# One transformer block on one core: K and Q stored in operand order, the softmax output's DMAs moved to GpSimd's queue, and the end of the program reordered

## The chip, the core and the metric

The program runs on one core of a Trainium2 chip. The metric is the device time of one execution in microseconds (us); the profiler's span, from the first to the last instruction, is given beside it. Engines are named as in the profile: PE is TensorE (PEld its weight loads), DVE is VectorE, ACT is ScalarE, POOL is GpSimd, SP is SyncE, which here only issues DMAs.

## What is computed

A block with modulated layer norms, 2048 rows (S) of 512 (D), attention with 32 heads of 16, and a gated feed-forward of 1792 (F), all in float32:

```python
def _A_ref(x, wqkv, wo):
    ...
    scores = jnp.einsum("bhqd,bhkd->bhqk", q, k) * scale
    p = _softmax(scores, axis=-1)
    o = jnp.einsum("bhqk,bhkd->bhqd", p, v)
    return (lambda x, *d: x.transpose(*d))(o, 0, 2, 1, 3).reshape(B, S, D) @ wo

def _B_ref(x, w_gate, w_up, w_down):
    g = _silu(x @ w_gate)
    u = x @ w_up
    return (g * u) @ w_down
...
h = _layernorm(x, axis=-1) * (1 + ca) + sa
x = x + ga * _A_ref(h, A_wqkv, A_wo)
h = _layernorm(x, axis=-1) * (1 + cb) + sb
x = x + gb * _B_ref(h, B_w_gate, B_w_up, B_w_down)
```

The six vectors sa to gb come from silu(c) @ w_mod.

## The kernel before

**Products in three terms.** Every float32 operand of the projections and the feed-forward is split into a high part and a rest (a cast, then a subtraction), and a product is the sum high·high + high·rest + rest·high. The scores do the same inside one matmul: 48 of its partitions hold, for each of a head's 16 numbers, three rows, (high, rest, high) for K and (high, high, rest) for Q; two more rows (ones in K, the negated maximum in Q) subtract the maximum.

**Projections (up to the first score).** For each of the four chunks of 512 rows the kernel normalizes, transposes and modulates x, and computes Q and K transposed and V. `proj_T` (L358) copies a bank into `prt` (high and rest) and stores it with one DMA (L370) to the DRAM tensors `qd` and `kd`, which are two planes, high and rest. `load_parts` (L398) brings a group of four heads back as operand rows: three row blocks times two partition halves are six DMAs of 16 partitions each, `kop` for K (2048 columns, three tiles in turn) and `qop` for Q (512 columns).

**Attention.** The work is cut into 32 units: unit u is chunk u // 8 of the queries and head group u % 8 (four heads). A unit has 16 steps, one for each block of 128 keys; a step has four score matmuls (L504, exponential on ACT at L506) and four matmuls for the row maximum of a later unit (L477, maximum on DVE at L479). A score and a maximum matmul use different halves of PE's rows and run side by side. The maxima run `LEAD` = 20 steps ahead, so the first maximum of unit u+2 is due in unit u, at its 14th step. The probabilities times V (`pv_step`, L519) fill one bank per unit, `banks[7]`; its last row of every head is the softmax's denominator.

**From the pv bank to the out projection.** When a unit ends (`close_unit`, L808), ACT copies the bank to `o` in two halves (L523). Then a chain follows, step by step from the list `due`: the denominators go by DMA to `dn` (L529), DVE inverts them (L533), they go to DRAM `d_dr` (L534) and come back over all partitions as `rb` (L539); POOL multiplies (L545), and the product goes to `o_dr` (L546). Once the last unit of a chunk is through, `load_o` (L646) loads the chunk's `oT` and `split_o` (L651) splits it on POOL; the out projection reads it. All these DMAs stand in SP's queue, which issues in order: while one waits for its data, nothing behind it is issued. K and Q loads, two DMAs at each step (`before`, L821), the feed-forward's weights (L639, L644) and the splitting of those weights during the first 124 steps (`split_weights`, L573) are in the same queue.

**Plain and filled steps.** The order on every engine is written by hand (no scheduler): the program order of the Python code is the order of each engine's queue. In `plain` only attention runs. In `filled` (L899) each two steps carry 12 more pairs of matmuls with 64 rows from the previous chunk's work (`LONG`, `SHORT` say how many terms go after each score), then six half steps of pv. A chunk's work is the out projection (4 `filled`), the second norm and its transposes (`turned`, L681, 2 `filled`), and then 14 gate-up jobs of two `filled` and 14 down jobs of one. It begins at the steps `STARTS` = 138, 267, 396. A gate-up job ends with tanh on ACT, two products on DVE and a split to `mid` on POOL (L746 to L754), which the down job reads (L706).

**The end.** The third chunk keeps its last six jobs (`KEEP`) for after the attention. There `whole` runs them in full rows (L714) between the links of the last unit's chain; then come `load_o`, `split_o`, the last out projection, the norm and the last chunk's feed-forward (L957 to L998).

**The clock.** The profile gives the clock that TensorE was granted in a stretch (PEclk, 1.00 is full).

Of the kernel before, what the change touches and what calls it, by code (L numbers as in the profile page):

```python
# [102 lines left out]
def block_kernel(ctx, tc, x, wqkv, wo, w_gate, w_up, w_down, c, w_mod, out):  # L103
# [27 lines left out]
    qd = dram.tile([2, D, S], F32, name="qd")  # L131
    kd = dram.tile([2, D, S], F32, name="kd")
# [225 lines left out]
    def proj_T(ci, w, m):  # L358
        def job():
# [3 lines left out]
            def post():  # L363
# [5 lines left out]
                dst = (qd, kd)[w][:, m * P:(m + 1) * P, ci * CW:(ci + 1) * CW].rearrange("r p s -> p r s")  # L369
                nc.sync.dma_start(dst, prt.bitcast(F32))  # L370
# [27 lines left out]
    def load_parts(dst, src, parts, g, c0, c1):  # L398
        for r, part in enumerate(parts):
            heads = src[part, g * 64:(g + 1) * 64, c0:c1].rearrange("(s b d) c -> b d s c", s=2, b=2)  # L400
            for b in range(2):
                nc.sync.dma_start(dst[64 * b + 16 * r:64 * b + 16 * r + 16].bitcast(F32), heads[b])
                yield

    def load_k0(ci):
        run(load_parts(kop[0][:, :, ci * CW:(ci + 1) * CW], kd, KPARTS, 0, ci * CW, (ci + 1) * CW))

# [43 lines left out]
    stored, posts = set(), []  # L451
# [8 lines left out]
    def load_k(u):  # L460
        return load_parts(kop[u % 3], kd, KPARTS, u % NG, 0, S)

    def load_q(u):
        ci, g = divmod(u, NG)
        qop[u] = pb.tile([P, 2, CW], F32R, name="qop", tag="qop", bufs=3)
        return load_parts(qop[u], qd, QPARTS, g, ci * CW, (ci + 1) * CW)

# [40 lines left out]
    def pv_step(i, half):  # L508
# [13 lines left out]
        if kt == 15:  # L522
            nc.scalar.copy(o_[u][:, cols], pv[u][:, cols])  # L523

    def out_a(u):
# [3 lines left out]
        nc.sync.dma_start(dn, o[16:P:32, :].rearrange("h (b e) -> h b e", e=16))  # L529
        return o, dn  # L530

    def out_b(u, o, dn):
        nc.vector.reciprocal(dn, dn)  # L533
        nc.sync.dma_start(d_dr[u].rearrange("h (b e) -> (h b) e", e=16), dn)  # L534
        return o,

    def out_r(u, o):
        rb = pf.tile([P, CW], F32, name="rb", tag="rb", bufs=1)
        nc.sync.dma_start(rb, d_dr[u][:, None, :].to_broadcast([4, 32, CW]))  # L539
        return o, rb  # L540

    def out_c(u, o, rb):
# [3 lines left out]
        nc.sync.dma_start(o_dr[ci, g], on)  # L546
        stored.add(u)
# [69 lines left out]
    class Chunk:  # L617
        def __init__(self, ci, x2, oT, hT):
# [10 lines left out]
            nc.sync.dma_start(self.x2, xd[:, 4 * ci:4 * ci + 4, :])  # L629
# [16 lines left out]
        def load_o(self):  # L646
            for k in range(NK):
                src = o_dr[self.ci, 2 * k:2 * k + 2].rearrange("g (h e) s -> (g h) e s", e=32)[:, 0:DH, :]
                nc.sync.dma_start(self.oT[1][:, k, :].bitcast(F32), src)
# [334 lines left out]
    for t in range(4):  # L984
        ch.normalize(t)
# [36 lines left out]
```

## Time and profile before

| | |
|---|---|
| Time, median of 3 runs | 2179.66 us (2170.13 to 2184.38) |
| The profiled execution | 2185.03 us; its span 2183.2 us |
| First score, last scores (L504) | 198.73 us, 1987.56 us from the span's start |
| Busy: PE, DVE, ACT, POOL | 1964.7, 1571.5, 1263.3, 317.2 us |
| Granted TensorE clock, mean | 0.94 |
| DMA | 261.21 MB, 120 GB/s; SP's queue took 48.4% of 16 engines' span |

PE is busy 90% of the span, but a share over the whole span says little here: the three stages have different limits, and a matmul at half clock counts as busy twice as long. So the page is only the start, and the stretches are read one by one: how long 16 steps last, what PE waited for, and what clock it had.

### The profile page before, as it was taken

The numbers are of one execution on the slowest core, as the hardware profiler recorded it, in microseconds if no ns is written. First come the engines' busy times: TensorE is split into PE (matmuls) and PEld (weight loads), VectorE is DVE, ScalarE is ACT, GpSimd is POOL, SyncE is SP. The second block draws the span as 40 slices with busy tenths as digits, with TensorE's granted clock in tenths as the row PEclk, the third lists the DMA queues.
The fourth block names the chain that finished last, engine by engine and source line by source line (L and its number), as shares of the span: only waits on it lengthen the run. The fifth ranks groups of instructions, "written<-read, shape, count | busy, mean of one in ns | idle before, by whom it ended". The sixth has DMA issues, their size and how long they took to land. (4 is left out here: it accounts for less than half of the span.)

```text
span 2183.2 us, 40914 instructions
## 1 busy us (share of the span) xinstructions
PE 1964.7 (90%) x16860; PEld 1176.5 (54%) x16860; DVE 1571.5 (72%) x2666; ACT 1263.3 (58%) x2330; POOL 317.2 (15%) x301
## 2 busy tenths in 40 slices
PE   7998977888978998999968999999979999897799
PEld 5764433333434665665434666665444466565587
DVE  5467977778867887888856888888867988741333
ACT  3223866667756665666746666666757766663100
POOL 2001233332011100110011101100011010011222
PEclk9998998889889999999988999999988999999899
DMA  8776566565344454434534545443532445224443
GB/s 244 198 162 115 112 179 176 138 182 150 48 124 105 92 108 117 118 95 83 111 60 98 124 110 114 106 98 79 118 79 41 84 108 110 97 93 146 173 174 116
DMA packets 90175, 261.21 MB, mean 120 GB/s; under 512 B 20252, under 2 KB 32540, under 8 KB 69116
## 3 DMA queue, kind: packets, MB, share of 16 engines
q1 hardware_dynamic: 88836, 258.06, 48.4%
q8 instruction: 133, 2.18, 0.5%
q10 hardware_dynamic: 1152, 0.52, 0.1%
q14 instruction: 54, 0.44, 0.1%
HBM read 203.82 MB, written 53.74 MB: 118 GB/s over the span
## 5 line engine op out<-in xcount | busy, mean ns | idle before, releaser
L479 DVE TENSOR_REDUCE mx<-bank 128x1 f32<-128x512 f32 x2048 | 1304.1, 685 | 354.1 <-PE bank L477 201.3
L477 PE MATMUL bank<-kop,qop 48*128 48x512 f32 x2048 | 804.9, 452 | 63.0 <-DMA kop<-kd 28.8
L504 PE MATMUL bank<-qop,kop 50*128 50x512 f32 x2048 | 800.4, 446 | 35.1 <-ACT pt__6232 L506 1.6
L504 PEld LDWEIGHTS bank<-qop,kop 50*128 50x128 f32 x2048 | 364.8, 191 | 366.1 <-issue 75.6
L477 PEld LDWEIGHTS bank<-kop,qop 48*128 48x128 f32 x2048 | 360.1, 192 | 96.4 <-issue 62.0
L706 PE MATMUL bank<-act,wgu 64*128 64x512 f32 x1920 | 305.7, 395 | 8.5 <-DMA wgu<-gu_dr 8.5
L706 PEld LDWEIGHTS bank<-act,wgu 64*128 64x128 f32 x1920 | 191.6, 189 | 43.0 <-issue 9.3
L545 POOL TENSOR_TENSOR on<-o,rb 128x512 f32<-128x512 f32 x32 | 41.0, 1280 | 811.8 <-DMA rb<-d_dr 378.6
L706 PE MATMUL bank<-wd,mid 64*128 64x512 f32 x912 | 151.1, 397 | 2.1 <-DMA wd<-wd_dr 1.5
L753 POOL CAST mid<-m 128x512 fp32r<-128x512 f32 x56 | 34.3, 612 | 678.6 <-DVE m L752 672.4
L706 PEld LDWEIGHTS bank<-wd,mid 64*128 64x128 f32 x912 | 96.6, 188 | 15.9 <-POOL mid L753 1.8
L208 PE MATMUL bank<-hT,wqs 128*128 128x512 f32 x384 | 97.1, 404 | 3.7 <-DVE prt L367 2.4
L750 DVE SCALAR_TENSOR_TENSOR q<-th,bank 128x512 f32<-128x512 f32 x56 | 38.1, 681 | 86.0 <-ACT th L746 86.0
L746 ACT ACTIVATE th<-bank 128x512 f32<-128x512 f32 x56 | 33.5, 599 | 113.5 <-PE bank L714 79.2
L706 PE MATMUL bank<-wgu,act 64*128 64x512 f32 x288 | 54.4, 439 | 42.6 <-POOL act L654 41.0
L208 PEld LDWEIGHTS bank<-hT,wqs 128*128 128x128 f32 x384 | 71.5, 191 | 26.2 <-issue 5.9
L754 POOL TENSOR_TENSOR mid<-m,mid 128x512 fp32r<-128x512 f32 x56 | 72.3, 1291 | 4.5
L765 DVE TENSOR_TENSOR x<-bank,x 128x512 f32<-128x512 f32 x84 | 54.2, 683 | 25.9 <-PE bank L706 17.5
L714 PE MATMUL bank<-kop,kop 128*128 128x512 f32 x240 | 60.5, 410 | 8.6 <-ACT kop L654 8.5
L706 PEld LDWEIGHTS bank<-wgu,act 64*128 64x128 f32 x288 | 31.5, 203 | 54.5 <-POOL act L654 44.1
L714 PEld LDWEIGHTS bank<-kop,kop 128*128 128x128 f32 x240 | 46.7, 197 | 21.5 <-ACT kop L654 11.0
L367 DVE TENSOR_TENSOR prt<-bank,prt 128x512 fp32r<-128x512 f32 x32 | 22.0, 689 | 46.9 <-ACT prt L365 46.9
(6246 smaller groups left out, 5131.9 us busy)
## 6 DMA issues: line engine op xcount, KB each, us to landing
kop<-kd SPq DMA_DIRECT2D x192, 256.0 KB
wgu<-gu_dr SPq DMA_DIRECT2D x48, 1024.0 KB
wd<-wd_dr SPq DMA_DIRECT2D x28, 1024.0 KB
gu_dr<-wgu SPq DMA_DIRECT2D x14, 1024.0 KB
qop<-qd SPq DMA_DIRECT2D x198, 64.0 KB
kd<-prt SPq DMA_DIRECT2D x16, 512.0 KB
qd<-prt SPq DMA_DIRECT2D x16, 512.0 KB
rb<-d_dr SPq DMA_DIRECT2D x32, 256.0 KB
```

What stands on the lines that cost most here:

```text
L208: nc.tensor.matmul(pt, lhs(a, k), rhs(b, k), start=(n == 0), stop=(n == 3 * nk - 1))
L477: nc.tensor.matmul(pm, qop[u][rows, s, qt * P:(qt + 1) * P], kop[u % 3][rows, s, kc * CW:(kc + 1) * CW], start=True, stop=True)
L479: nc.vector.tensor_reduce(mx[u][:, b, s, qt, kc:kc + 1], pm, op=ALU.max, axis=AX.X)
L504: nc.tensor.matmul(sp, kop[u % 3][rows, h // 2, kt * P:(kt + 1) * P], qop[u][rows, h // 2, :], start=True, stop=True)
L545: nc.gpsimd.tensor_mul(on, o, rb)
L706: nc.tensor.matmul(outs[e], lhs(e, a, k)[rows], rhs(b, k)[rows], start=(ph == 0 and j == 0), stop=(ph == 1 and j == z))
L714: nc.tensor.matmul(outs[e], lhs(e, a, k), rhs(b, k), start=(j == 0), stop=(j == z))
L746: nc.scalar.activation(th, outs[0], AF.Tanh, scale=0.5)
L750: nc.vector.scalar_tensor_tensor(q, th, 1.0, outs[0], op0=ALU.add, op1=ALU.mult)
L753: nc.gpsimd.tensor_copy(mid[:, 0, :], m32)
L754: nc.gpsimd.tensor_sub(mid[:, 1, :], m32, mid[:, 0, :].bitcast(F32))
L765: nc.vector.tensor_add(ch.x2[:, t, :], outs[e], ch.x2[:, t, :])
```

## The change

`qd` and `kd` become [D, 3, S]: a row of D holds its three operand rows next to each other. `proj_T` writes high and rest with one DMA and the second copy of the high part with another. `load_parts` then needs one DMA of 48 partitions for each partition half, two instead of six. The loads of unit u+2 no longer go out two DMAs at a step from unit u's second step on, Q first: K is issued whole right behind the last score of unit u-1, whose tile it takes, and Q one step later; the loads for unit 1 come three steps earlier and once (before they stood in the program twice), those for unit 2 before step 0. The five kinds of DMA of the chain from `o` to `oT`, and the output stores of the first three chunks, move to POOL's queue; the product comes one step earlier, and `load_o` and `split_o` too. The chunks' work begins at steps 141, 267 and 399, so that every `filled` covers an odd step and the even one after it; `LONG` puts its terms after the first six scores; in `filled` the bank is copied to `o` in one piece.

At the end, seven jobs are kept instead of six. The last chunk's tiles are set up 24 steps before the end, and the three quarters of its `oT` that are complete are loaded and split then, on POOL. After the last pv, `out_terms` runs 36 of the last out projection's 48 matmuls first; the other 12 follow after 44 matmuls of the kept jobs. Of the kept jobs 32 matmuls come between the norm and its transposes, and four weight tiles are loaded ahead instead of three.

The core of the diff:

```diff
-KEEP = 6
-KWIN = 34
-STARTS = (138, 267, 396)
-LONG = (0, 2, 2, 2, 2, 2, 2, 0)
+KEEP = 7
+REST = 30
+STARTS = (141, 267, 399)
+LONG = (2, 2, 2, 2, 2, 2, 0, 0)
-KPARTS = (0, 1, 0)
-QPARTS = (0, 0, 1)
...
-    qd = dram.tile([2, D, S], F32, name="qd")
-    kd = dram.tile([2, D, S], F32, name="kd")
+
+    qd = dram.tile([D, 3, S], F32, name="qd")
+    kd = dram.tile([D, 3, S], F32, name="kd")
...
-                dst = (qd, kd)[w][:, m * P:(m + 1) * P, ci * CW:(ci + 1) * CW].rearrange("r p s -> p r s")
-                nc.sync.dma_start(dst, prt.bitcast(F32))
+                dst = (qd, kd)[w][m * P:(m + 1) * P, :, ci * CW:(ci + 1) * CW]
+                nc.sync.dma_start(dst[:, 1 - w:3 - w, :], prt.bitcast(F32))
+                nc.sync.dma_start(dst[:, 2 * w, :], prt[:, 0, :].bitcast(F32))
...
-    def load_parts(dst, src, parts, g, c0, c1):
-        for r, part in enumerate(parts):
-            heads = src[part, g * 64:(g + 1) * 64, c0:c1].rearrange("(s b d) c -> b d s c", s=2, b=2)
-            for b in range(2):
-                nc.sync.dma_start(dst[64 * b + 16 * r:64 * b + 16 * r + 16].bitcast(F32), heads[b])
-                yield
+    def load_parts(dst, src, g, c0, c1):
+        heads = src[g * 64:(g + 1) * 64, :, c0:c1].rearrange("(s b d) r c -> b (d r) s c", s=2, b=2)
+        for b in range(2):
+            nc.sync.dma_start(dst[64 * b:64 * b + KR].bitcast(F32), heads[b])
...
-        if kt == 15:
+        if kt == 15 and by_halves:
+        elif kt == 15 and half:
+            nc.scalar.copy(o_[u], pv[u])
...
-        nc.sync.dma_start(dn, o[16:P:32, :].rearrange("h (b e) -> h b e", e=16))
+        nc.gpsimd.dma_start(dn, o[16:P:32, :].rearrange("h (b e) -> h b e", e=16))
...
-        nc.sync.dma_start(rb, d_dr[u][:, None, :].to_broadcast([4, 32, CW]))
+        nc.gpsimd.dma_start(rb, d_dr[u][:, None, :].to_broadcast([4, 32, CW]))
...
-        nc.sync.dma_start(o_dr[ci, g], on)
...
+        nc.gpsimd.dma_start(o_dr[ci, g], on)
...
-        def load_o(self):
-            for k in range(NK):
+        def load_o(self, ks=range(NK)):
+            for k in ks:
-                nc.sync.dma_start(self.oT[1][:, k, :].bitcast(F32), src)
-
-        def split_o(self, alone=False):
-            for k in range(NK):
+                nc.gpsimd.dma_start(self.oT[1][:, k, :].bitcast(F32), src)
+
+        def split_o(self, ks=range(NK), alone=False):
+            for k in ks:
...
+    def add_o(ch, t0, outs):
...
+    def out_terms(ch, t, pt, ks):
+        for k in ks:
+            for a, b in ((0, 0), (0, 1), (1, 0)):
+                nc.tensor.matmul(pt, ch.oT[a][:, k, t * P:(t + 1) * P], ch.wo[k // 2][:, b, k % 2, :],
+                                 start=(k == 0 and a == b == 0), stop=(k == NK - 1 and a == 1))
...
-                    nc.sync.dma_start(od[:, 4 * ch.ci + t, :], ch.x2[:, t, :])
+                    (nc.sync if ch.ci == last else nc.gpsimd).dma_start(od[:, 4 * ch.ci + t, :], ch.x2[:, t, :])
...
-            at(i + 5, lambda: out_c(u, *res.pop(u)))
+            at(i + 4, lambda: out_c(u, *res.pop(u)))
-                at(i + 6, lambda: chunks[u // NG].load_o())
-                at(i + 7, lambda: chunks[u // NG].split_o())
-
-    loads = []
+                at(i + 5, lambda: chunks[u // NG].load_o())
+                at(i + 6, lambda: chunks[u // NG].split_o())
...
-        u, kt = divmod(i, 16)
-        if kt == 1 and 1 <= u + 2 < NU:
-            loads.append(chain(load_q(u + 2), load_k(u + 2)))
-        for _ in range(2):
-            while loads and next(loads[0], loads) is loads:
-                loads.pop(0)
+
+        u, kt = divmod(i + 1, 16)
+        if 1 <= u and u + 2 < NU:
+            if kt == 0:
+                load_k(u + 2)
+            if kt == 1:
+                load_q(u + 2)
...
+            load_k(2)
+            load_q(2)
...
-        if i == -LEAD + 6:
-            loads.append(chain(load_k(1), load_q(1)))
-        before(i)
+        if i == -LEAD + 3:
+            load_k(1)
+            load_q(1)
...
-            pvs((HALVES[(w - 2) % 4] if done > 8 else 0) + (w == 4 * steps // WIN - 1))
+            pvs((HALVES[(w - 2) % 4] if done > 8 else 0) + (w == 4 * steps // WIN - 1), True)
...
-    def filled(places, work, tail=None):
+    def filled(places, work, tail=None, pairs=8):
...
-            bank, places = Turn(4, 5, 0), ALONE[places]
-        for r in range(8):
+            bank, places = Turn(4, 5, 0), ALONE.get(places, places)
+        for r in range(pairs):
-        pvs(6)
+        pvs(6, False)
...
+    def two_of(u):
+        return [kop[u % 3][:, e, :].rearrange("p (k c) -> p k c", k=NK) for e in range(2)]
+
+    def begin_last():
+        chunks[last] = ch = Chunk(last, v_flat[:, 0:4 * D].rearrange("p (t d) -> p t d", t=4), two_of(NU - 2),
+                                  two_of(NU - 1))
+        ch.load_wo([kop[(NU - 3) % 3][:, k, :].rearrange("p (b k d) -> p b k d", b=2, k=2) for k in range(NK // 2)])
+
+    at(n - 24, begin_last)
+    at(n - 13, lambda: chunks[last].load_o(range(NK - 1)))
+    at(n - 11, lambda: chunks[last].split_o(range(NK - 1)))
...
-            plain(n - done // 4 - 2 * KWIN)
+            plain(REST)
...
+    filled(none, iter(()), pairs=4)
...
-    pairs = [(0, 1), (2, 3), (4, 5)]
-        return [banks[b] for b in pairs[turn_n % len(pairs)]]
+        return [(banks[4], banks[5]), (banks[6], banks[7])][turn_n % 2]
...
-    room = [v_flat[:, 4 * D * e:4 * D * (e + 1)].rearrange("p (t d) -> p t d", t=4) for e in range(2)]
-    oT, hT = ([kop[u % 3][:, e, :].rearrange("p (k c) -> p k c", k=NK) for e in range(2)] for u in (NU - 2, NU - 1))
-    ch = Chunk(last, room[0], oT, hT)
-    ch.load_wo([kop[(NU - 3) % 3][:, k, :].rearrange("p (b k d) -> p b k d", b=2, k=2) for k in range(NK // 2)])
-    chp = chunks[last - 1]
+    ch, chp = chunks[last], chunks[last - 1]
+    ch.load_x2()
+    for t in range(4):
+        out_terms(ch, t, banks[t], range(NK - 1))
+        if t == 1:
+            res[NU - 1] = out_b(NU - 1, *res[NU - 1])
+        if t == 3:
+            res[NU - 1] = out_r(NU - 1, *res[NU - 1])
+    take(rest, 12)
+    out_c(NU - 1, *res.pop(NU - 1))
-    res[NU - 1] = out_b(NU - 1, *res[NU - 1])
+    ch.load_o((NK - 1,))
-    res[NU - 1] = out_r(NU - 1, *res[NU - 1])
-    take(rest, 10)
-    out_c(NU - 1, *res.pop(NU - 1))
+    ch.split_o((NK - 1,), True)
-    ch.load_o()
-    take(rest, 12)
-    ch.split_o(True)
-    take(rest, 6)
-    for t0 in (0, 2):
-        run(out_pair(ch, t0, two(), False))
-        hook()
+    for t in range(4):
+        out_terms(ch, t, banks[t], (NK - 1,))
+        if t % 2:
+            add_o(ch, t - 1, banks[t - 1:t + 1])
-    ch.nt = [room[1][:, 2 * k:2 * k + 2, :] for k in range(2)]
+    ch.nt = [v_flat[:, (4 + 2 * k) * D:(6 + 2 * k) * D].rearrange("p (t d) -> p t d", t=2) for k in range(2)]
+    take(rest, 32)
-    ch.ahead = 3
-    take(rest, 12)
-    for kk in range(NK // 2):
-        run(ch.turned([banks[6], banks[7]], kk))
-        hook()
-        take(rest, 8)
-    run(rest)
+    ch.ahead = 4
+    for kk in range(NK // 2):
+        run(ch.turned(banks[2 * kk:2 * kk + 2], kk))
+        hook()
+        take(rest, 12)
+    run(rest)
```

Three places show the order of instructions. **SP's queue in unit 1**, where K and Q of unit 3 are loaded (`kop_86` is the tile of units 0, 3, 6, and so on). Before:

```order
L402 DMA qop<-qd 16x2x512 x4
L577 DMA mid<-in_B_w_down 128x2x512
L402 DMA qop<-qd 16x2x512 x2
L534 DMA d_dr<-dn 128x16
L539 DMA rb<-d_dr 128x1x512
L402 DMA kop_86<-kd 16x2x2048 x6
L546 DMA o_dr<-on 128x512
```

and with the change:

```order
L584 DMA wo_dr<-wgu 128x2048
L576 DMA mid<-in_A_wo 128x2x512
L401 DMA kop_86<-kd 48x2x2048 x2
L401 DMA qop<-qd 48x2x512 x2
L584 DMA wo_dr<-wgu 128x2048
```

The links of unit 0's chain (`d_dr`, `rb`, `o_dr`) stood before and behind K in the queue; now none is in it, and K stands ahead of Q.

**POOL's queue at the end of the first chunk's units** (units 5 to 7), where the out projection's operand is made (`act_5528` and `act_5457` are the tile `oT`). Before:

```order
L581 CAST wd<-mid 128x1024
L582 TENSOR_TENSOR wd<-mid,wd 128x1024
L545 TENSOR_TENSOR on<-o,rb 128x512 x3
L654 CAST act_5527<-act_5528 128x512
L655 TENSOR_TENSOR act_5528<-act_5528,act_5527 128x512
```

and with the change (units 6 and 7):

```order
L546 DMA o_dr<-on 128x512
L529 DMA dn<-o 128x1x16
L534 DMA d_dr<-dn 128x16
L539 DMA rb<-d_dr 128x1x512
L545 TENSOR_TENSOR on<-o,rb 128x512
L546 DMA o_dr<-on 128x512
L650 DMA act_5457<-o_dr 128x1x512 x4
L655 CAST act_5456<-act_5457 128x512
L656 TENSOR_TENSOR act_5457<-act_5457,act_5456 128x512
```

Where POOL held one product for a unit, it now holds the whole chain in order, four DMAs and the product, and the four loads of `oT`.

**PE's queue after the last pv matmul** (`bank_70` is the pv bank). Before, from the last pv matmul to the first kept jobs, then the out projection:

```order
L519 MATMUL bank_70<-pt__20836,v_flat 32x256
L714 MATMUL bank_65<-act_16074,wgu 128x512
L714 MATMUL bank_65<-act_16075,wgu 128x512
L714 MATMUL bank_65<-act_16074,wgu 128x512 x2
L714 MATMUL bank_65<-act_16075,wgu 128x512
...
L714 MATMUL bank_67<-kop_1421,kop_86 128x512 x12
```

and with the change:

```order
L517 MATMUL bank_70<-pt__20533,v_flat 32x256
L742 MATMUL bank_63<-kop_1412,kop_86 128x512 x9
L742 MATMUL bank_64<-kop_1412,kop_86 128x512 x9
L742 MATMUL bank_65<-kop_1412,kop_86 128x512 x9
L742 MATMUL bank_66<-kop_1412,kop_86 128x512 x9
L715 MATMUL bank_69<-act_15861,wgu 128x512
...
L742 MATMUL bank_63<-kop_1412,kop_86 128x512 x3
```

Before, 60 matmuls of kept jobs ran ahead of the whole out projection (48, the rows with `kop_1421`); now 36 of those 48 come first and need nothing of the last two units.

More of the change, by code (lines that the diff above doesn't have):

```diff
@@ L450, in block_kernel @@
     qop, mx, pts, pv, o_, due, res = {}, {}, {}, {}, {}, {}, {}
-    stored, posts = set(), []
+    posts = []
     n = 16 * NU
@@ L460, in load_k @@
     def load_k(u):
-        return load_parts(kop[u % 3], kd, KPARTS, u % NG, 0, S)
+        load_parts(kop[u % 3], kd, u % NG, 0, S)
     def load_q(u):
@@ L802, in block_kernel @@
     ones_rows(1)
-    run(load_q(0))
+    load_q(0)
     take(late, 22)
@@ L957, in block_kernel @@
     for i, half in halves:
-        pv_step(i, half)
+        pv_step(i, half, False)
     after(n - 1)
```

48 lines of the change are left out of this document (24 added, 24 removed).

## Prediction

> **What bounds the kernel now.** The page comes first, and only as a warning.
>
> ```profile
> span 2183.2 us, 40914 instructions
> PE 1964.7 (90%) x16860; PEld 1176.5 (54%) x16860; DVE 1571.5 (72%) x2666; ACT 1263.3 (58%) x2330; POOL 317.2 (15%) x301
> ```
>
> PE leads, but a matmul at half clock counts double, so I read stretches instead: score matmuls (L504) in chosen windows, four to a step; the last three columns are clock, DMA share and GB/s.
>
> ```profile
> 198.70:593.00 394.30, 191.61 (x513) 91.91 (x513) 0.88 0.59 143
> 1669.80:1711.50 41.70, 22.78 (x66) 10.60 (x64) 1.00 0.39 62
> 700.00:800.00 100.00, 44.11 (x108) 18.99 (x108) 1.00 0.39 104
> ```
>
> The first row is the plain start, 128 steps in 394.3 us, 3.08 each. The second is one plain unit at full clock, 16 steps in 41.7 us, 2.61 each. The third is filled, 27 steps in 100 us, 3.70 each. So the start loses 394.3 - 8 x 41.7 = **60.7 us** against the kernel's own clean unit. The waits of PE there say why:
>
> ```profile
> PE bank L477 <- DMA kop<-kd: 24.5, 3, 14.6
> PE bank L477 <- DMA gu_dr<-wgu: 8.8, 1, 8.8
> PE bank L477 <- issue: 7.7, 1, 7.7
> ```
>
> All three are the first maximum of a new unit, which needs the unit's K (the names in the last two rows are only what ended near it). The waits make 41 us; the rest is the clock, 0.88 against 1.00. One unit shows what makes K late, SP's queue and then PE:
>
> ```profile
> 549.45 0.56 SPq L529 DMA_DIRECT2D dn<-o  x1
> 550.12 4.20 SPq L402 DMA_DIRECT2D qop<-qd  x6
> 556.94 0.34 SPq L534 DMA_DIRECT2D d_dr<-dn  x1
> 558.37 0.55 SPq L539 DMA_DIRECT2D rb<-d_dr  x1
> 558.96 2.85 SPq L402 DMA_DIRECT2D kop<-kd  x6
> 580.44 0.76 PE L477 MATMUL bank<-kop,qop 48*128 48x512 f32 x1 [3.81 <-DMA kop<-kd]
> ```
>
> K's tile was free near 544, its DMAs went out at 558.96, behind Q and the chain, and landed only near 580. The windows of all engines for that transfer and for weight loads over 128 partitions:
>
> ```profile
> 559.00:580.00 21.00, 17.63 (x175) 8.39 (x171) 18.78 (x32) 16.09 (x32) 1.28 (x1) 1.00 0.79 100
> 2062.00:2082.00 20.00, 20.00 (x83) 16.32 (x82) 5.27 (x8) 1.80 (x3) 5.72 (x6) 0.93 0.59 249
> ```
>
> 100 GB/s at a share of 0.79 against 249 at 0.59: loads to 16 partitions hold the DMA engines 3.3 times as long for a byte. Two faults, then: a late issue (some 15 us) and a slow transfer (some 20).
>
> **After the first chunk** the waits of PE (600 to 1989) name another place.
>
> ```profile
> PE bank L706 <- POOL act L654: 41.0, 3, 16.0
> PE bank L519 <- ACT o L523: 17.8, 33, 0.9
> PE bank L706 <- DMA wgu<-gu_dr: 8.5, 2, 4.9
> 612.00:640.00 28.00, 12.38 (x102) 6.71 (x100) 10.62 (x18) 8.69 (x16) 7.54 (x9) 0.70 0.58 111
> 1095.00:1123.00 28.00, 11.36 (x88) 6.01 (x90) 8.54 (x15) 7.09 (x14) 8.66 (x9) 0.70 0.57 92
> 1577.00:1602.00 25.00, 14.70 (x117) 8.32 (x115) 11.51 (x19) 8.57 (x16) 8.65 (x9) 0.80 0.35 76
> ```
>
> Three out projections wait 41.0 us for the split operand, and the clock stays at half a little longer. The chain of the second one, on SP and POOL:
>
> ```profile
> 1075.08 0.57 SPq L529 DMA_DIRECT2D dn<-o  x1
> 1083.87 0.34 SPq L534 DMA_DIRECT2D d_dr<-dn  x1
> 1088.76 0.55 SPq L539 DMA_DIRECT2D rb<-d_dr  x1
> 1102.38 1.26 POOL L545 TENSOR_TENSOR on<-o,rb 128x512 f32<-128x512 f32 x1 [48.01 <-DMA rb<-d_dr]
> 1104.05 9.43 SPq L649 DMA_DIRECT2D act<-o_dr  x4
> 1114.24 0.61 POOL L654 CAST act<-act 128x512 fp32r<-128x512 f32 x1 [10.60 <-DMA act<-o_dr]
> 1114.93 1.27 POOL L655 TENSOR_TENSOR act<-act,act 128x512 fp32r<-128x512 f32 x1
> ```
>
> From 1075 to 1114, 39 us, of which the small transfers `d_dr` (4.9) and `rb` (13.6) queue with 3 MB of x and weights.
>
> **The end**, two windows and three stalls of PE:
>
> ```profile
> 1991.40:2059.70 68.30, 45.07 (x164) 32.24 (x160) 20.47 (x49) 9.87 (x15) 13.03 (x14) 0.81 0.41 136
> 2059.70:2183.20 123.50, 118.48 (x504) 96.12 (x504) 38.69 (x56) 8.41 (x14) 26.75 (x28) 0.98 0.45 176
> 2017.42 3.34 PE L714 MATMUL bank<-kop,kop 128*128 128x512 f32 x6 [6.99 <-ACT kop L654]
> 2041.83 0.48 PE L686 MATMUL bank<-ident,v_flat 128*128 128x128 f32 x1 [4.46 <-ACT v_flat L678]
> 2059.74 4.60 PE L714 MATMUL bank<-kop,wgu 128*128 128x512 f32 x10 [6.27 <-DMA wgu<-gu_dr]
> ```
>
> In the second window a matmul takes 118.48 / 504 = 0.235 us. The first holds 144 such and 16 transposes, about 36 us of work in 68.3.
>
> **The change part by part**, against the span of 2183.2. *K and Q.* K goes out right behind the score that frees its tile, with nothing of the chain ahead. Its transfer is bounded by 1.57 MB at 249 GB/s, 6.3 us, and by the 20 us of now; two blocks of 48 partitions are nearer to the wide loads, so I take 8. Its first maximum is due 13 steps later, 34 us: even 20 us fit, and 14 more are left for a store of split weights that SP waits for. So the 60.7 us go, whichever bound holds, unless something new is late. That is POOL: in the start it splits weights, and now holds the chain too.
>
> ```profile
> 198.70:593.00 394.30, 338.66 (x3051) 151.11 (x3050) 317.05 (x544) 272.69 (x535) 112.45 (x90) 0.88 0.59 143
> ```
>
> 112.45 us in 334 would be 34%, more while it splits; its 90 operations take 1.25 us each and are issued three or four at a time, so `dn` can stand behind some 5 us of splitting, and DVE's reciprocal, which waits for `dn`, is due only two steps, 5.2 us, after it. What is queued behind that reciprocal on DVE are the maxima, four to a step, that PE's banks wait for. I charge 0 to 2 us for each of eight units, 5 in all (bound 16): **-56**. K waits later in the run: **-4**.
>
> *Out projections.* `d_dr` and `rb` leave the queue of the big loads. No row shows a DMA on POOL's queue; the nearest are the same transfers in the unit above, `d_dr` 558.37 - 556.94 = 1.4 us, and in this chain 4.9 and 13.6. I take 3 and 5. From the end of the pv bank that makes 5.2 us to the reciprocal, 3 for `d_dr`, 5 for `rb`, 1.3 for the product, 3 and 4 for the store and load of the `oT` quarters, 0.6 for the first cast, and 2 for issuing: 24 us instead of 39. The first cast is needed after 10.5 steps of 2.5 us (26 us) in the first chunk, 9.3 (23) in the second, 13.3 (33) in the third. So the second still waits, with splits of 1.9 us a quarter behind the first one, about 3 us. Of 41.0 and some 8 for the clock I take **-44** (bounds -49 and -15).
>
> *Filled.* Weight loads no longer stand behind the chain: 8.5 us and the clock after them, **-10** (0 to -18). One copy instead of two spares PE part of 17.8 us, but odd groups put the maximum's two DMAs on ACT into the middle of a filled group: **-3** (-12 to +8). Four filled steps become plain, 4 x (3.70 - 2.61): **-4**.
>
> *The end.* 24 matmuls more, 168 in all, 39.5 us and 2 for transposes. The last unit's chain, with the links just used but no steps to wait for (copy 0.6, `dn` 3, 3, 5, 1.3, 3, 4, cast and subtraction 1.3), takes 21 us and has 36 + 44 matmuls over it, 18.8 us; the norm has 32 (7.5 us, against the 4.46 now waited), the split after the transposes 44. I leave 10 us of stalls: 52 instead of 68, **-17** (-25 to -3).
>
> *Before the first score.* PE waits there once, and DMA is nearly full early on:
>
> ```profile
> PE bank L477 <- DMA qop<-qd: 6.6, 1, 6.6
> 40.00:100.00 60.00, 60.00 (x291) 48.13 (x290) 28.55 (x54) 16.82 (x30) 0.00 (x0) 1.00 0.84 228
> ```
>
> The second load of unit 1, which caused the 6.6, is gone; 32 more stores of 256 KB are new, half of them in that window: 4 MB on 13.7 would ask 0.84 x 1.3 = 1.09 of the engines, 6 us too much, hidden in part by four `prt` buffers. **-4** (-10 to +12).
>
> Sum: -56 - 4 - 44 - 10 - 3 - 4 - 17 - 4 = **-142**. The profiled execution took 2185.0 in all, 1.8 outside the span and 5.4 above the median; from the median, 2179.7 - 142 = **2038 us**.
>
> A rule speaks against the chain's new place. The Trainium skill, DMA: Bandwidth & Descriptors, section Latency and other measured facts, gives a first byte after about 1 us on GpSimd's path and 0.6 on SP's. By it five links would be 2 us longer, and my estimate of the sum 2 us higher, since only the second out projection is short of time. No row here shows it, and nothing above hangs on it.
>
> **The rivals.** *K is issued in time but SP is not free*: stores that wait for POOL's splits stand ahead of K for over 14 us, and half of the 56 stays. For it: SP's 23 stores of split weights are in that stretch; against it: its greatest waits there are the chain's,
>
> ```profile
> SPq L529 <- ACT o L523: 72.0, 4, 21.8
> SPq L546 <- POOL on L545: 48.8, 7, 11.9
> ```
>
> About 2068; chance 0.12.
>
> *The chain on POOL is no shorter*, since the same 16 DMA engines serve it and `rb` takes 13.6 us again: the out projections keep waiting for 30 of the 44, the end for 8 of the 17: about 2076; chance 0.14. For it: the share of 0.57 in the second window while `rb` crept. Against it: in the unit above `rb` was sent at a quiet moment and nobody waited for it. The Trainium skill states it as a rule (DMA: Bandwidth & Descriptors, Issuing engines are not separate DMA queues): all queues share the engines, and a second one saves only the issue.
>
> *POOL's queue becomes the bound*, the slower side: POOL waits in order for `d_dr` and `rb`, 4.9 + 13.6 = 18.5 us as in the chain above. A `mid` behind them (0.61 + 1.27) has two filled groups, 14.8 us, until a down job reads it; beyond 13 us of waiting each us stops PE, 5.6 x 17 units = 95 us, and in 15 plain units a late `dn` stops DVE's maxima, some 8 us each, 120. 2038 + 215 = about 2250. Against it: POOL waited as long for `rb` before (48.01 in the row) and no down job suffered. Chance 0.06.
>
> *The waits go but the time does not*: DVE (busy 317.05 of 394.3 us already in the slow start) or the clock set a pace near 3 us a step, and the clean unit was an exception; about 2165, chance 0.07. Against it: that unit has DVE in the same work at 2.61.
>
> **How the numbers follow.** The forecast has 0.61, with 2005 to 2070 of its own. With the first two rivals the range is **2000 to 2100**. Three runs of before lie within 0.7%, so 1% is about what can be told from no change: faster 0.61 + 0.12 + 0.14 + 0.02 = 0.89, same 0.05, slower 0.06.
>
> **What would show it.** Right: 128 steps from the first score in about 340 us with no K wait over 2 us; K landing within 10 us of its issue; out projections waiting under 5 us in sum; clock over 0.97; under 55 us from the last pv to the last chunk's first gate-up. Wrong: DVE waiting for `dn` over 2 us in many units, PE waiting for `mid`, or a later first score.

## The result and the profile after

The changed kernel takes **2092.6 us** (median of 4 runs, 2086.9 to 2097.7) against 2179.4: a ratio of 0.961, with a 95% interval of 0.956 to 0.965. Forecast were 2038, 2000 to 2100. So the time lies in the range, and of the 142 us of the sum 87 came. The profiled execution took 2095.9, span 2093.7.

First the page of the changed kernel, then its windows of all engines: the 128 steps from the first score, the rest up to the last score, and the stretch from the last pv to the last chunk's first gate-up matmul. The last three columns are again clock, DMA share and GB/s.

```profile
span 2093.7 us, 40510 instructions
PE 1960.2 (94%) x16836; PEld 1185.0 (57%) x16836; DVE 1579.0 (75%) x2663; ACT 1251.8 (60%) x2306; POOL 422.4 (20%) x463
```

```profile
185.60:548.60 363.00, 336.54 (x3047) 149.84 (x3048) 318.54 (x543) 271.95 (x534) 131.19 (x118) 0.92 0.58 156
548.60:1903.70 1355.10, 1286.07 (x12286) 777.82 (x12282) 1086.97 (x1805) 909.10 (x1650) 230.00 (x275) 0.96 0.41 102
1906.20:1970.20 64.00, 46.86 (x186) 36.92 (x186) 18.68 (x47) 8.60 (x13) 18.85 (x23) 0.84 0.40 149
```

The 128 steps took 363.0 us; before they took 394.3, and about 340 were forecast. PE's busy time there stayed what it was (338.66 before, 336.54 now), and the clock rose from 0.88 to 0.92 only. The third row holds 64.0 us where under 55 were forecast (68.3 before).

Next the waits of PE in the changed kernel (us in total, times, longest), and below them DVE's for `dn`:

```profile
PE bank L475 <- DVE mx L477: 30.0, 24, 7.3
PE bank L715 <- DVE q L757: 7.8, 1, 7.8
PE bank L742 <- ACT kop L655: 6.0, 1, 6.0
PE bank L707 <- POOL act L655: 2.9, 1, 2.9
PE bank L475 <- DMA kop<-kd: 0.8, 1, 0.8
```

```profile
DVE dn L533 <- DMA dn<-o: 50.6, 19, 10.5
```

The old waits are gone: K 0.8 us, the out projections 2.9 instead of 41.0. A new one has come. PE waits 30.0 us for banks that DVE has not read, and DVE stands 50.6 us, in 19 of 32 units (10.5 of it in the last), before a reciprocal of a quarter of a microsecond, because `dn` has not landed. The prediction had named this wait, over 2 us in many units, as a sign of being wrong; it is that long in 7. In the kernel before that wait occurred once, 4.0 us, in the end:

```profile
DVE dn L533 <- DMA dn<-o: 4.0, 1, 4.0
```

One unit of the changed kernel, from the timelines of SP, POOL and DVE:

```profile
505.49 1.80 SPq L401 DMA_DIRECT2D kop<-kd  x2
507.39 0.86 SPq L401 DMA_DIRECT2D qop<-qd  x2
...
512.16 0.71 POOL L529 DMA_DIRECT2D dn<-o  x1 [18.05 <-ACT o L521]
...
511.91 7.27 DVE L477 TENSOR_REDUCE mx<-bank 128x1 f32<-128x512 f32 x12 [1.10 <-PE bank L475]
520.70 0.25 DVE L533 RECIPROCAL dn<-dn 128x16 f32<-128x16 f32 x1 [1.52 <-DMA dn<-o]
```

POOL is not held up here: it issues `dn` 0.3 us after the end of the copy it waits for, as in most units (2.6 us at most). But K and Q went out 5 to 7 us earlier. What the DMA engines did from 505 to 519 us (the row DMA is their busy share in 40 slices, in tenths; below it SP's queue with packets, MB and share; last the time from issue to landing), and then the same in a late unit with no K left to load, from 1801 to 1812 us:

```profile
DMA  0000979499989389599497955979959949999989
q1 hardware_dynamic: 437, 1.96, 91.8%
dn<-o POOLq DMA_DIRECT2D x1, 8.0 KB, 8.5
```

```profile
DMA  0000000000000710000000000000000000000000
dn<-o POOLq DMA_DIRECT2D x1, 8.0 KB, 2.3
```

The same 8 KB take 8.5 us beside 1.96 MB of K and Q, and 2.3 alone. That made **theory A**: `dn` is late because K and Q, now issued just before it, hold the DMA engines. **Theory B**: GpSimd's queue is slow for this transfer, which SP's queue never was. A third, C: the slow first halves of the plain units (their first eight steps take 21 to 30 us, in the kernel before 19 to 22) come from something else that falls in the same time, such as the clock.

### The profile page after: what moved, and what is told of

The parts are those of the page before. It is cut to its first block, busy times and chain, and to the rows that moved or that the text cites. A ratio compares the mean times of both kernels' runs of the same rounds, so it can differ in the third digit from the quotient of the medians.

```text
span 2093.7 us, 40510 instructions
## 1 busy us (share of the span) xinstructions
PE 1960.2 (94%) x16836; PEld 1185.0 (57%) x16836; DVE 1579.0 (75%) x2663; ACT 1251.8 (60%) x2306; POOL 422.4 (20%) x463
## 4 chain that ended last, share of the span: by engine, by line
PE 63%; DMA 12%; DVE 10%; issue 6%; ACT 4%; POOL 3%; ACTq 1%; SPq 0%; POOLq 0%; DVEq 0%
PE bank L517 16%; PE bank L707 14%; PE bank L502 13%; DMA dn<-o 8%; DVE mx L477 7%; PE bank L715 6%; PE bank L475 6%; PE bank L207 6%; DMA rb<-d_dr 1%; DMA mid<-in_B_w_gate 1%; ACTq L494 1%; POOL wgu L581 0%; PE bank L687 0%; POOL mid L761 0%; DMA d_dr<-dn 0%
## 5 line engine op out<-in xcount | busy, mean ns | idle before, releaser
L502 PE MATMUL bank<-qop,kop 50*128 50x512 f32 x2048 | 810.1, 447 | 50.3 <-ACT pt__6239 L504 2.2
L475 PE MATMUL bank<-kop,qop 48*128 48x512 f32 x2048 | 821.0, 452 | 31.8 <-DVE mx L477 30.0
L502 PEld LDWEIGHTS bank<-qop,kop 50*128 50x128 f32 x2048 | 369.5, 191 | 385.6 <-issue 79.1
L475 PEld LDWEIGHTS bank<-kop,qop 48*128 48x128 f32 x2048 | 365.2, 191 | 73.5 <-DVE mx L477 51.3
L707 PEld LDWEIGHTS bank<-act,wgu 64*128 64x128 f32 x1872 | 204.6, 187 | 33.9 <-DVE m L759 3.3
L707 PEld LDWEIGHTS bank<-wd,mid 64*128 64x128 f32 x912 | 100.2, 188 | 19.3 <-DVE m L759 3.2
L529 POOL DMA_DIRECT2D dn<-o x32 | 22.7, 711 | 384.0 <-ACT o L523 182.7
L715 PE MATMUL bank<-wd,mid 128*128 128x512 f32 x216 | 56.7, 419 | 12.5 <-DVE q L757 7.8
L534 POOL DMA_DIRECT2D d_dr<-dn x32 | 18.2, 568 | 198.6 <-DVE dn L533 198.6
L715 PEld LDWEIGHTS bank<-wd,mid 128*128 128x128 f32 x216 | 43.0, 201 | 24.7 <-DVE q L757 8.3
```

The source lines that it names most:

```text
L475: nc.tensor.matmul(pm, qop[u][rows, s, qt * P:(qt + 1) * P], kop[u % 3][rows, s, kc * CW:(kc + 1) * CW], start=True, stop=True)
L502: nc.tensor.matmul(sp, kop[u % 3][rows, h // 2, kt * P:(kt + 1) * P], qop[u][rows, h // 2, :], start=True, stop=True)
L707: nc.tensor.matmul(outs[e], lhs(e, a, k)[rows], rhs(b, k)[rows], start=(ph == 0 and j == 0), stop=(ph == 1 and j == z))
L715: nc.tensor.matmul(outs[e], lhs(e, a, k), rhs(b, k), start=(j == 0), stop=(j == z))
```

## The experiments

All ratios are against runs of the kernel before on the same chip (medians 2181.0 to 2185.3). Stage times below are of one profiled execution each; where nothing was changed they differ by up to 10 us between kernels.

**K later in the program** tells A from B by moving K.

```
-            if kt == 0:
+            if kt == 6:
                 load_k(u + 2)
-            if kt == 1:
+            if kt == 7:
                 load_q(u + 2)
```

> The changed kernel, with K's loads at the 7th step of a unit and Q's at the 8th instead of the first and second; dn stays on GpSimd's queue. Theory A (dn lands 8.7 us after its issue because the 1.5 MB of K and Q are issued beside it and fill the DMA engines): dn lands in 1.5 to 3 us, DVE's waits for dn (50.6 us) fall under 10 us, PE's 30.0 us for banks held by DVE go, first halves of plain units fall from 24 to about 20 us, and the time is 2045 to 2065 us. Theory B (GpSimd's queue is slow for this transfer of 64-byte pieces): dn still lands after 7 to 10 us, and the time is 2085 to 2100. If K now comes too late for its first maximum, PE waits for K show it.

Measured: 2084.5 us, ratio 0.956 (0.952 to 0.960), no difference from the change that can be told. The edit did only half of what it should. SP issues a load as soon as its tile is free and nothing stands ahead of it, so in half of the units K still went out ahead of `dn`; in the others something before it on SP had to wait. That makes two groups inside one execution. Landing of `dn` (min, median, max, in us from issue) in the changed kernel, and in this one:

```profile
DMA to landing us min/median/max: 2.1/8.7/11.4
```

```profile
DMA to landing us min/median/max: 2.0/5.1/12.1
```

Two units of this kernel, each with its issues from the timeline and the landing of its `dn`: the first with K issued after `dn`, the second with K before it.

```profile
603.42 0.69 POOL L529 DMA_DIRECT2D dn<-o  x1 [15.01 <-ACT o L523]
612.56 0.90 SPq L401 DMA_DIRECT2D kop<-kd  x2
```

```profile
dn<-o POOLq DMA_DIRECT2D x1, 8.0 KB, 2.0
```

```profile
1427.65 1.72 SPq L401 DMA_DIRECT2D kop<-kd  x2
1434.90 0.71 POOL L529 DMA_DIRECT2D dn<-o  x1 [0.47 <-ACT o L523]
```

```profile
dn<-o POOLq DMA_DIRECT2D x1, 8.0 KB, 10.4
```

In the trace `dn` landed within 2.4 us in 13 of 32 units here, and in 2 of the changed kernel's, both after the last K. GpSimd's queue is not slow by itself: B falls. The time did not follow, since DVE still waited 35.2 us and Q or K came late to PE once, 6.2 us.

**`dn` alone on another queue**, ACT's or SP's, the second behind K and Q.

```
-        nc.gpsimd.dma_start(dn, o[16:P:32, :]...)
+        nc.scalar.dma_start(dn, o[16:P:32, :]...)     (or nc.sync)
```

> The changed kernel, with the load of dn alone on ACT's queue; K and Q are issued beside it as before. Theory A (the shared DMA engines): dn still takes 6 us or more, DVE still waits over 30 us for it, time 2080 to 2100. Theory B (GpSimd's queue): dn in about 2 us, DVE's waits gone, 2045 to 2065.

> The changed kernel, with the load of dn alone back on SP's queue, where it is issued right behind the K and Q loads of the same unit. Theory A: it lands with or behind them, 6 us or more, DVE waits as in the changed kernel or longer, time 2080 to 2105. Theory B: about 2 us as in the kernel before, DVE's waits gone, 2045 to 2065.

Measured: ACT 2141.7 us, ratio 0.982 (0.978 to 0.985); SP 2066.3, ratio 0.945 (0.941 to 0.950). DVE's waits for `dn`, of ACT's queue and then of SP's:

```profile
DVE dn L533 <- DMA dn<-o: 72.1, 20, 9.4
```

```profile
DVE dn L533 <- DMA dn<-o: 28.3, 9, 9.0
```

On no queue is `dn` in time in every unit beside K, which is A's answer, but the queues are not equal: ACT's run was slower than either theory allowed, SP's faster than A did, and by its time alone nearer to B. In the 29 units with K beside it the last packet of `dn` ended a median of 5.4 us after the issue on SP's queue and 9.4 on ACT's; on GpSimd's it landed after 8.7. Why, beside the same K, it is later from one queue than from another stays open.

**The reciprocal two steps later**, and the chain behind it; K and `dn` as in the change.

```
-            at(i + 2, ... out_b)   i + 3 out_r   i + 4 out_c   i + 5 load_o   i + 6 split_o
+            at(i + 4, ... out_b)   i + 5 out_r   i + 6 out_c   i + 7 load_o   i + 8 split_o
```

> The changed kernel, with the reciprocal and everything behind it in the chain two steps later (about 5 us), K and dn as they are. Both A and B: dn still lands 7 to 10 us after its issue, but DVE's waits for it fall from 50.6 to under 10 us, PE's waits for banks held by DVE go, and the time is 2045 to 2070, of which up to 8 us is given back at the out projections. Theory C (the slower first halves come from something else that falls in the same time, such as the clock): the waits go and the time stays within 1% of 2093.

Measured: **2039.8 us**, ratio 0.935 (0.932 to 0.939). Its landing of `dn`, its wait for it, its 128 steps and its out projections:

```profile
DMA to landing us min/median/max: 2.0/8.6/11.5
```

```profile
DVE dn L533 <- DMA dn<-o: 18.2, 2, 11.2
```

```profile
188.20:524.60 336.40, 317.58 (x3051) 144.50 (x3050) 316.55 (x544) 271.16 (x535) 130.94 (x118) 0.97 0.63 168
```

```profile
PE bank L707 <- POOL act L655: 9.2, 2, 6.2
```

`dn` lands as late as before (8.6 us), nobody waits for it in the loop but once, and 53 us are gone. The first halves of the plain units take 19 to 21 us again but for one unit (27.2). So the reciprocal's wait is the cost, and C falls. The edit moves the rest of the chain too, but the next run speaks against that as the help: there the reciprocal stays in its place, DVE waits no more in the loop, and the 128 steps come down as well.

In this execution 26.6 us of the 128 steps went, 19 of them (336.54 - 317.58) out of the busy time of the same matmuls, with the clock at 0.97 instead of 0.92. Two kernels below are the same up to the 128th step and took 344.9 and 346.3 us there; the first of them:

```profile
186.50:531.40 344.90, 327.51 (x3051) 147.59 (x3050) 316.02 (x544) 271.49 (x535) 130.78 (x118) 0.95 0.62 164
```

So the stall costs 17 to 27 us there, and about half of that or more is busy time at a lower clock. In the changed kernel four of these steps' six waits for `dn` have a stretch at half clock that begins in them or up to 2.5 us behind them; other such stretches have no wait for `dn` beside them.

**`dn` first**: `dn` on SP, and K and Q behind it.

```
-        nc.gpsimd.dma_start(dn, ...)
+        nc.sync.dma_start(dn, ...)
...
-            if kt == 0: load_k   if kt == 1: load_q
+            if kt == 3: load_k   if kt == 4: load_q
```

> The changed kernel, with dn on SP's queue and the loads of K and Q moved behind it (fourth and fifth step of a unit), so that dn starts on engines that K does not yet hold. The rest of the chain stays on GpSimd's queue, and the reciprocal where it was. Theory A (dn is late because K and Q hold the DMA engines): dn in 2 to 3 us except where a store of split weights stands before it, DVE's waits for it under 12 us in all, the first 128 steps in 335 to 345 us, time 2030 to 2045. If something else slows the first halves of plain units, as with dn on SP behind K: 2060 to 2070.

Measured: 2071.7 us, ratio 0.946 (0.941 to 0.951). A's waits went, the forecast time did not come:

```profile
DVE dn L533 <- DMA dn<-o: 6.7, 1, 6.7
```

```profile
PE bank L707 <- POOL act L655: 19.3, 3, 10.9
```

The 128 steps took 344.5 us, as A said. But K now flies beside the next small transfer, `rb`: its median from issue to landing rose from 5.0 us in the changed kernel to 6.1. In the three units whose out projection waits, `on` comes 28.6, 26.6 and 26.5 us after the copy (21.4, 19.7 and 21.1 in the changed kernel), and the out projections wait 19.3 us. The burst now delays the small link that shares its 13 us. That is a part of what is missing only: from the 128 steps to the last score it took 1348.2 us against 1321.0 with the later reciprocal. Some 10 of these 27 us are in the waits for the operand and the others in busy time, at a clock of 0.96 instead of 0.98; what else lowered the clock was not traced.

**The loads of K and Q in three pieces of 16 partitions**, on the kernel with the later reciprocal.

```
-            nc.sync.dma_start(dst[64 * b:64 * b + KR]..., heads[b])
+            for r in range(0, KR, 16):
+                nc.sync.dma_start(dst[64 * b + r:64 * b + r + 16]..., heads[b][r:r + 16])
```

> The kernel with the later reciprocal, and each load of K and Q cut into three of 16 partitions, as before the change; order and place stay. The prediction's premise (13 steps, 34 us, are enough even for the slow transfer; the order of issue is what counts): no PE wait for K over 2 us, time within 1% of 2040. If 48 partitions at once are what counts: K takes over 20 us, PE waits for it, dn and rb land later still, time 2060 to 2110.

Measured: 2079.1 us, ratio 0.951 (0.947 to 0.955). Windows over one such burst, in pieces of 16 partitions, and of 48 in the changed kernel:

```profile
513.00:532.00 19.00, 18.11 (x190) 8.33 (x190) 17.88 (x31) 16.16 (x32) 1.26 (x2) 1.00 0.82 98
```

```profile
507.00:521.00 14.00, 12.69 (x131) 5.58 (x129) 11.34 (x20) 12.06 (x25) 0.71 (x1) 1.00 0.89 133
```

The waits of the kernel with pieces of 16:

```profile
PE bank L476 <- DVE mx L478: 19.0, 12, 12.8
PE bank L476 <- DMA kop<-kd: 1.9, 1, 1.9
```

```profile
DVE dn L534 <- DMA dn<-o: 25.0, 5, 13.3
```

K itself is in time even so (1.9 us), as the prediction said, and yet one load of 48 partitions instead of three of 16 is worth 39 us (2079.1 - 2039.8). That the longer burst holds others up longer fits `dn`, which lands after a median of 10.6 us instead of 8.6. But PE's waits in the rows above are only 9 us longer than with the later reciprocal (19.0 after 11.9, and 1.9 after none), so where most of the 39 us goes is not shown.

**K and Q alone**, and **the chain on GpSimd's queue alone**, each put into the kernel before.

```
 kernel before
+ qd, kd as [D, 3, S]; load_k, load_q over 48 partitions, at kt == 0 and 1
```

> The kernel before, with K and Q alone as in the change (rows in operand order, 48 partitions at once, issued at the start of a unit); the chain stays whole on SP's queue, behind K. Theory A: K's waits of PE (41 us in the first 128 steps) go, but dn lands behind K in SP's queue and DVE waits for it, so the first 128 steps take 360 to 370 us, as with dn alone on SP; the out projections' 41 us stay or grow: 2120 to 2160. If dn's place on GpSimd's queue were the cause, the first 128 steps would take about 340 us and the whole 2105 to 2125.

```
 kernel before
+ dn, d_dr, rb, o_dr, loads of oT: nc.sync -> nc.gpsimd
```

> The kernel before, with the chain alone (dn, d_dr, rb, the store of o, the loads of oT) on GpSimd's queue; K and Q keep their layout, their 16-partition loads and their place. As the prediction has it (the queue of the chain is what the out projections wait for): their 41.0 us fall under 10, K goes out some 5 us earlier in a unit, and the time is 2115 to 2135. If the loads of K and Q are what makes the chain slow whatever its queue (the two-queue rival, and the run with K and Q alone, in which those waits fell to 11.7 us with the chain on SP): waits of 20 us and more stay, dn is late beside Q and K, time 2150 to 2185.

Measured: K and Q alone 2085.5 us, ratio 0.954 (0.950 to 0.957); the chain alone 2134.8, ratio 0.980 (0.975 to 0.985). Their waits for the out projections' operand and for `dn`, K and Q first:

```profile
PE bank L705 <- POOL act L653: 11.7, 3, 5.6
DVE dn L532 <- DMA dn<-o: 18.5, 12, 3.9
```

```profile
PE bank L706 <- POOL act L654: 10.8, 2, 6.3
DVE dn L533 <- DMA dn<-o: 57.7, 12, 7.6
```

Either part alone takes the out projections' 41.0 us down to 11 or so, and PE's waits for K, 28.8 us in the whole kernel before, to 0.8 and 1.6. They are two cures for one fault, loads of 16 partitions ahead of the chain on one queue, and their gains (about 100 and 46 us) do not add: both together, with the other edits of the change, give 87. Moving the chain also brings the late `dn`, 57.7 us: on SP it had gone out ahead of the unit's K and Q and was safe from them. For K and Q alone I had expected 2105 at best; the missed point was that the out projections' wait was theirs too.

**The chain back on SP's queue**, with the change's K and Q and the later reciprocal; the output stores stay on GpSimd's.

```
- dn, d_dr, rb, o_dr, loads of oT: nc.gpsimd
+ nc.sync
```

> The kernel with the later reciprocal, and the whole chain back on SP's queue. If GpSimd's queue is worth what the prediction gave it once dn may be late: out projections wait 25 us and more, the end is 5 us longer, time 2060 to 2080. If the gain is K's and the reciprocal's place alone: 2035 to 2050, out projections wait under 12 us as in the kernel with K and Q alone.

Measured: **2036.0 us**, ratio 0.933 (0.929 to 0.937), not to be told from 2039.8 with the chain on GpSimd's. Its one wait of that kind:

```profile
PE bank L707 <- POOL act L655: 4.7, 1, 4.7
```

Once K and Q are short and the reciprocal late, this pair shows no worth in the chain's queue. The Trainium skill (DMA: Bandwidth & Descriptors, Issuing engines are not separate DMA queues) says that transfers from any issuer run on the same 16 engines, and that a second issuer saves little beyond the issuing; this pair of runs agrees. A second pair, the two sums below, leans to SP.

**The end in another order**, on the kernel with the later reciprocal.

```
     ch.split_o((NK - 1,), True)
-    take(rest, 12)
+    take(rest, 16)
+    hook()
...
-    take(rest, 32)
+    take(rest, 28)
```

> The kernel with the later reciprocal, and in the end the last four matmuls of a gate-up job and its tanh, product and split put ahead of the last quarter of the out projection instead of behind it. If PE's 7 us stall there is a pair of banks that DVE has not read because its product stands behind the 20 small operations of the norm, that stall goes, and the time is 5 to 8 us less than with the later reciprocal alone (2040), 2032 to 2036. If the out projection's last quarter sets the end anyway, the stall moves behind it and the time stays at 2037 to 2042.

Measured: 2038.7 us, ratio 0.932 (0.928 to 0.937): by the times nothing can be told. In the profile the stall went. PE in the end, of the changed kernel and then of this one:

```profile
1930.71 4.75 PE L742 MATMUL bank<-kop,kop 128*128 128x512 f32 x12 [5.99 <-ACT kop L655]
...
1946.97 5.12 PE L715 MATMUL bank<-wd,mid 128*128 128x512 f32 x12 [7.84 <-DVE q L757]
...
1970.19 11.36 PE L715 MATMUL bank<-kop,wgu 128*128 128x512 f32 x48
```

```profile
1884.85 5.49 PE L742 MATMUL bank<-kop,kop 128*128 128x512 f32 x12 [5.46 <-ACT kop L655]
1890.13 5.98 PE L715 MATMUL bank<-wd,mid 128*128 128x512 f32 x24
...
1916.91 8.40 PE L715 MATMUL bank<-kop,wgu 128*128 128x512 f32 x36
```

The down job's second pair needs banks that hold a gate-up's result until DVE's product has read them, and that product stood behind the norm. With the product ahead of the norm the 7.84 us are gone, and from the last score to the end it is 180.9 us instead of 189.6 with the later reciprocal. That execution's 128 steps, which the edit does not touch, were 8.5 us slower.

**Two sums.** The reordered end and later reciprocal, with the first two out projections started three steps later (`STARTS = (144, 270, 399)`); then the same with the chain on SP.

> The kernel with the later reciprocal and the reordered end, and the first two out projections started three steps later (144 and 270 instead of 141 and 267), so that the 6.9 us that they still wait for the operand go. Expected 2024 to 2034; if the wait was hidden in what follows, 2035 to 2041.

> All that helped, together: K and Q as in the change, the whole chain on SP's queue with the reciprocal two steps later, the reordered end, the first two out projections three steps later. With the chain on SP, the end was 4.7 us shorter than on GpSimd's queue and one out projection waited 4.7 us; the reordered end took 8.7 us off and the later start of the out projections about 7. If these add up: 2015 to 2028. If the later start is not needed with SP (its plain steps are only moved) and the two gains of the end are one: 2026 to 2036.

Measured: 2031.5 us, ratio 0.931 (0.927 to 0.935), and **2018.0 us** (5 runs, 2016.5 to 2021.1), ratio 0.925 (0.922 to 0.927). The second beats the change by 75 us and the kernel before by 164. The two differ in the chain's queue alone, and here SP's is 13 us faster, with intervals that just touch; of the 16 us between the profiles 13 lie in the 128 steps (346.3 and 333.0), a stage that alone differs by 10 between like kernels. So a small gain for SP's queue is likely, and not shown. The second's 128 steps, and its stretch from the last pv to the last chunk:

```profile
186.80:519.80 333.00, 320.38 (x3049) 145.69 (x3050) 317.86 (x543) 271.03 (x534) 112.66 (x90) 0.97 0.65 170
1838.40:1893.10 54.70, 45.37 (x186) 35.06 (x186) 18.21 (x47) 8.73 (x13) 15.64 (x18) 0.94 0.50 179
```

## Why the prediction was right, and where it was not

Times by stage, from windows of one profiled execution each, in us:

| kernel | to first score | 128 steps | to last score | end | span |
|---|---|---|---|---|---|
| before | 198.7 | 394.3 | 1394.6 | 195.6 | 2183.2 |
| the sum's terms | -4 | -56 | -65 | -17 | -142 |
| after | 185.6 | 363.0 | 1355.1 | 190.0 | 2093.7 |
| K and Q alone | 186.6 | 356.4 | 1340.3 | 195.2 | 2078.5 |
| chain alone | 199.8 | 371.2 | 1367.6 | 187.7 | 2126.3 |
| later reciprocal | 188.2 | 336.4 | 1321.0 | 189.6 | 2035.2 |
| the same, chain on SP | 189.1 | 336.2 | 1327.2 | 184.9 | 2037.4 |
| all that helped | 186.8 | 333.0 | 1316.2 | 178.5 | 2014.5 |

(The -65 are K later in the run, the out projections, and the three items of the filled stretches: 4 + 44 + 10 + 3 + 4.)

**Right: side, range and first fault.** The range held by luck: its upper part was there for two rivals that did not come, and 2092.6 lies outside the forecast's own 2005 to 2070. K waited 24.5 us by name and 41 in all, and waits 0.8 now; the out projections' 41.0 are 2.9.

**The step that failed** is one term of the sum: "I charge 0 to 2 us for each of eight units, 5 in all (bound 16)", for the reciprocal that waits for `dn`. Against the kernel that moves only the reciprocal and what follows it, it cost 17 to 27 us in the 128 steps (by three kernels alike there) and, by the table, 34.1 after them, where I had charged nothing; 53 by the medians. What the reciprocal waits for, and the maxima queued behind it, were named rightly. The sum looked for a delay of `dn` on POOL's queue, behind splits, and there was one of 8 us, in a single unit of the kernel with the later reciprocal. The delay that counts is on the DMA engines.

**Why I missed it.** I put K at the unit's start for a gain, and left `dn` at the less than 2 us that it took when K went out behind it. The size failed with it: "nearer to the wide loads, so I take 8". K and Q moved at 133 GB/s at a share of 0.89, nearer to the 100 of before than to 249, and 1.96 MB held the engines for some 13 us: from 506 to 519 in the unit shown, with `dn` issued at 512.2. "Even 20 us fit" was true of K and beside the point. By its last packet K landed a median of 11.5 us after its issue, not within 10, and the clock was 0.958 instead of over 0.97.

**The out projections'** waits went, but the reason given was only one of two. It was put down to the chain leaving SP's queue, and that alone does take 41.0 to 10.8. K's and Q's loads alone do the same, to 11.7, with the chain left where it was: from the copy to the product it is then a median of 18.3 us, 24.4 before and 19.8 with the change. The stage after the 128 steps gave 39.5 us where the sum had 65, since the late `dn` costs there too.

**The end** gave 5.6 instead of 17. Two links of the last unit's chain, from the chain of waits:

```profile
1907.17 5.36 DMA dn<-o
...
1921.66 4.31 DMA o_dr<-on
```

I had 3 for each; from the last pv to the first waiting matmul it was 24.5 us (1906.2 to 1930.7) instead of 21, mostly by `dn`. The 10 us of stalls became 17 (6.0, 7.8, 2.7 and 0.6), by a wait that I did not have, 7.84 us for banks behind the norm on DVE; I had counted what covers the norm for PE, and not what else DVE owed. With the end reordered and the chain on SP it is 17.1 us shorter than before (178.5), the size of the term, by two edits that the change does not have.

**Before the first score** it was 13.1 us instead of 4. K and Q alone give 12.1 of it, the chain alone none: the 6.6 us of Q went, the clock up to there rose from 0.97 to 1.00, and the extra stores cost nothing to be seen.

**The rivals.** SP was free in time for K. The chain on POOL was shorter than before, though SP would have served. The slower rival had the right place, a late `dn` that stops DVE's maxima, but took POOL's queue for its cause and priced it at 120 us; it cost about half of that, the filled units included, and `mid` never stopped a down job before the end.

With the reciprocal moved, every stage but the end came to its term or better in that execution, and the sum to -148 (by the medians -140): the forecast of 2038 fits this change with one more edit in it. In part that is luck: the first stage and the third gave some 15 us more than their terms, the end 11 less.

## What to carry to other kernels

When a large load is moved ahead in time, list every small transfer that then starts inside its burst, and who waits for it in order: what a small transfer took before holds only beside what it ran beside. If the burst can't be moved, move the waiter, not the small transfer: another queue for `dn` gave between -26 and +49 us, a reciprocal two steps later -53. And two repairs of one wait don't add; run each alone before keeping both.

## What the runs showed of the hardware

An 8 KB transfer on GpSimd's queue lands 2.0 to 2.3 us after its issue when the engines are idle, and 5 to 11 (median 8.7) beside 2 MB of other loads. On SP's queue, issued behind the same loads, it ended after a median of 5.4 us, on ACT's after 9.4. In one window each, loads over 48 partitions moved 133 GB/s at a share of 0.89, over 16 partitions 98 at 0.82; so three times the partitions made them a third faster, not three times.
